# Unread identity products in the planned pauses of TensorE: a complex linear attention with a feed-forward behind it

## The chip, the cores and the metric

One core of one Trainium2 chip runs the whole program. The metric is the time of one execution in device microseconds (us). The kernel before took 697.37 us in the median of three runs (697.04 to 699.15). One more execution was profiled; every row of a trace below is from that one.

## The reference

For 4 batches and 8 heads, a state of 48x48 complex numbers runs over 768 time steps, and its output is the input of a two-layer feed-forward with GELU:

```python
mag = np.sqrt(a_re * a_re + a_im * a_im)
scale = np.minimum(mag, 0.999) / (mag + 1e-06)
a_re_n, a_im_n = (a_re * scale, a_im * scale)
for t in range(S):
    new_re = ar * S_re - ai * S_im
    new_im = ar * S_im + ai * S_re
    S_re, S_im = (new_re + kv, new_im)          # kv = k v^T of step t
    y[:, :, t] = np.einsum('bhd,bhde->bhe', q[:, :, t], S_re)
...
h = x @ w_in                                    # x: 3072 x 384, w_in: 384 x 2048
g = 0.5 * h * (1.0 + erf(h * inv_sqrt2))
return (g @ w_out).astype(np.float32)           # w_out: 2048 x 384
```

## The kernel before, in words

The recurrence is cut into chunks of time. The work has these parts, and the code names each of them:

- **lanes** (`tick`, `normalise`, `scan`, `squares_a`, `squares_b`, `logs`, `towards`, `against`): the factors `a` are normalised and multiplied up along time, slice by slice, in four groups of chunks. It is mostly work of VectorE (DVE) and ScalarE (ACT); its tiles are `a`, `tab`, `bt`, `tt` and `xt`. In the first group, `sum_of` lets TensorE (PE) add two squares: two products with the identity into a PSUM tile `att`, which ACT and DVE read. The results go to DRAM as `kq`.
- **weights** (`weights`): 32 pieces of the two weight matrices, 64-bit numbers that are split into a high part (`wi_hi`, `wo_hi`) and a low part (`wi_lo`, `wo_lo`). For each piece, PE subtracts in PSUM: identity times the rounded number, minus the high part, minus a correction. These three products in a row are called a triple here. Each triple goes into columns 0 to 383 of the same PSUM tile, `pos[BLK - 1]` (`po2`, one bank of 512 columns), and ACT or DVE copies the result out as `wi_lo` or `wo_lo`. So each triple must wait for the copy of the triple before it.
- **units** (`unit`): the attention of 128 time steps of one batch: loads of `kqn` and `vn`, transposes, scores, products with the state. The first two units come before the first block.
- **blocks** (`block`): the feed-forward, for two or three units at a time: `first` (`ph<-xT,wi_hi` and `wi_lo`), GELU on ACT, `second` (`po<-wo_hi,gh` and so on). Block `j0` is the first, `j1` the second. While a block is computed, the lanes, the weights and the units that later blocks need run beside it.

Nothing is issued as it is written: `Plan` records every operation as a step, and `Plan.order` puts the steps in order with a table of costs. Each step gets a planned engine, `s.start` and `s.cost`. `Plan.issue` (line 390) then issues them in that order, from one line, L399. So each engine has one fixed row of instructions, and each instruction waits in the row until what it needs is done. Waits between the engines are put in by the framework when an instruction is issued: it orders what touches the same tile where one of the two writes, and the rows in the section on the change show that it does so for `po2` as a whole, whatever columns of the bank are meant.

The planner doubles its cost of a PE step for some time after a pause, since PE runs at half of its clock then (`COLD`, `WARM` in `forward`). The planned times are used for nothing but the order.

The line of the code on which much of what follows rests, in `weights`, is:

```python
p = pos[BLK - 1][:, 0:DM]
```

Of the kernel before, what the change touches and what calls it, by code (L numbers as in the profile page):

```python
# [33 lines left out]
DM = H * D  # L34
# [4 lines left out]
BLK = max(BLOCKS)  # L39
# [45 lines left out]
TABLES = {AF.Ln: "natural_log_exp_and_others", AF.Exp: "natural_log_exp_and_others", AF.Gelu: "gelu"}  # L85
FIRST_TABLE = TABLES[AF.Ln]
NEAR = 0.076
LOCK = True
NGA, NGB = 4, 3
UPE = 6  # L90
# [18 lines left out]
class Plan:  # L109
# [78 lines left out]
    def ports(self, step, engine, calls):  # L188

        for call in calls:  # L190
            ins = [x for x in self.operands(call)[1] if x.tensor.space != PSUM and math.prod(c for _, c in x.ap[1:]) > 1]
            outs = self.operands(call)[0]
            if engine == "gpsimd" and ins or engine == "vector" and LOCK and (
                    len(ins) > 1 or ins and call[1] in ("tensor_scalar", "tensor_copy") and outs[0].tensor.space != PSUM):
# [79 lines left out]
    def forward(self, rank):  # L274
# [14 lines left out]
        while len(order) < len(steps):  # L289
            best = None  # L290
            for e, waiting in pool.items():
                if not waiting:
                    continue
                t = max(free[e], min(ready[i] for i in waiting)) + NEAR
                fits = [i for i in waiting if ready[i] <= t]
# [50 lines left out]
    def backward(self, end, taken, _):  # L346
# [8 lines left out]
        for _ in steps:  # L355
            best = None
            for e, waiting in pool.items():
                if not waiting:
                    continue
                t = min(free[e], max(ready[i] for i in waiting)) - NEAR  # L360
                i = last(i for i in waiting if ready[i] >= t)
# [25 lines left out]
            s.engine, s.start, s.cost, s.calls = e, start, cost, s.options[e][0]  # L387
        return [steps[i] for i in order]

    def issue(self):  # L390
        table = FIRST_TABLE
        self.nc.scalar.preload_act_table_set(table)
        for s in self.order():
            if s.table and s.table != table:
                table = s.table
                if table != "gelu":
                    self.nc.scalar.preload_act_table_set(table)  # L397
            for engine, name, args, kw in s.calls:
                getattr(getattr(self.nc, engine), name)(*args, **kw)  # L399

# [9 lines left out]
def lanes_and_chunks(ctx, tc, flags, a_lanes, x_lanes, v_units, w_in, w_out, out):  # L410
    nc = tc.nc
# [4 lines left out]
    P = Plan(nc, loose=[flags])  # L416
# [10 lines left out]
    ident = ident_r.bitcast(F32)  # L427
# [38 lines left out]
    pos = [ps.tile([128, 512], F32, name=f"po{i}", tag=f"po{i}")[:] for i in range(BLK)]  # L466
# [536 lines left out]
    for j, more in enumerate(BLOCKS[1:] + (0,)):  # L1003
# [6 lines left out]

        with P.work("blocks", f"j{j}"):
            block(j, between)
    P.issue()


def from_float64(nc, pool, src, out):
# [136 lines left out]
def tile_complex_linear_attention_moe(ctx, tc, q, k, v, a_re, a_im, w_in, w_out, a_lanes, x_lanes, v_units, w_pieces, out):  # L1153
# [9 lines left out]
    with ExitStack() as fast:  # L1163
        fast.enter_context(tc.manual_schedule())
        lanes_and_chunks(fast, tc, flags, a_lanes, x_lanes, v_units, w_pieces, w_out, out)
# [81 lines left out]
```

## Time and profile before

| | before |
|---|---|
| median of three runs | 697.37 us |
| profiled execution | 697.16 us |
| its span, from the first to the last instruction | 695.1 us |
| busy: PE, DVE, ACT | 638.8, 465.7, 459.3 us |
| mean granted clock of PE | 0.957 |

The 2.06 us between the span and the profiled execution's time are outside the program's instructions. PE is busy for 92% of the span, and the page's slices show where it isn't: in the first sixth. A row of a timeline gives the start, the time from the first to the last of a group, the engine, the line, the operation, what it writes and reads, its shapes, how many, and in brackets how long the engine sat idle before it and what it waited for. The products that take 32-bit numbers as they are (`po<-wh`, `att<-qT,kp`) leave two records each, the others one. Records of PE overlap, so the time of a piece of work is read from its start to the start of what follows at once.

### The profile page before, as it was taken

To read this page: it belongs to the slowest core of one execution; us is meant where nothing else is said; L and a number is where in the kernel's file an instruction comes from. 1 tells how busy PE (TensorE), PEld (TensorE's weight loads), DVE (VectorE), ACT (ScalarE), POOL (GpSimd) and SP (SyncE) were. 2 spreads that over 40 slices of the span, in tenths; PEclk is the share of its full clock that TensorE was granted. 3 is DMA by queue.
4 is the path that set the end of the run, shared out by engine and by line. 5 is a ranking of instruction groups with operands and counts; after the bars stand their busy time and mean duration, and the time that the engine had idled before them with its cause. 6 is when DMAs were issued, how large, how long until landed. Compare 5 with 4: busy or idle time off the path is not lost.

```text
span 695.1 us, 13858 instructions
## 1 busy us (share of the span) xinstructions
PE 638.8 (92%) x5138; PEld 588.3 (85%) x5138; DVE 465.7 (67%) x1154; ACT 459.3 (66%) x1118; POOL 31.9 (5%) x73
## 2 busy tenths in 40 slices
PE   3464799998999999999999999999999999999995
PEld 1232477996889999999889999999999999999995
DVE  5999988999999999999999973442332222131111
ACT  7777867999988788889899864454344333343332
POOL 1002110020000000300000000100000000000000
PEclk9865589999999999999999999999999999999998
DMA  8446936677455546637767555202322030010000
GB/s 303 138 136 176 301 110 165 203 199 234 134 150 148 148 119 183 180 95 217 206 198 212 118 133 149 83 20 72 113 76 61 5 103 1 1 44 4 24 1 26
DMA packets 112713, 86.68 MB, mean 125 GB/s; under 512 B 55680, under 2 KB 104960, under 8 KB 112640
## 3 DMA queue, kind: packets, MB, share of 16 engines
q1 hardware_dynamic: 112640, 85.75, 43.3%
q8 instruction: 41, 0.67, 0.4%
q14 instruction: 32, 0.26, 0.1%
HBM read 56.82 MB, written 23.59 MB: 116 GB/s over the span
## 4 chain that ended last, share of the span: by engine, by line
PE 75%; ACT 11%; DVE 10%; issue 2%; DMA 1%; SPq 0%; ACTq 0%; DVEq 0%
PE po L399 28%; PE ph L399 26%; PE att L399 20%; DVE a L399 2%; ACT tab L399 2%; DVE tt L399 1%; ACT wh L399 1%; ACT a L399 1%; DVE wh L399 1%; DVE xt L399 1%; ACT L399 1%; ACT L397 1%; DVE bt L399 1%; DVE tab L399 1%; ACT gh L399 1%
## 5 line engine op out<-in xcount | busy, mean ns | idle before, releaser
L399 PE MATMUL ph<-xT,wi_hi 128*128 128x384 f32 (+1 forms) x864 | 210.9, 326 | 0.3 <-ACT gf L399 0.3
L399 DVE TENSOR_TENSOR gl<-gf,gh 128x384 fp32r<-128x384 f32 (+1 forms) x143 | 72.9, 510 | 137.4 <-ACT gf L399 134.7
L399 PEld LDWEIGHTS ph<-xT,wi_hi 128*128 128x128 f32 x864 | 153.0, 188 | 3.1 <-ACT gf L399 0.6
L399 ACT ACTIVATE gh<-ph 128x384 fp32r<-128x384 f32 (+1 forms) x144 | 65.5, 455 | 134.3 <-PE ph L399 133.3
L399 PE MATMUL ph<-xT,wi_lo 128*128 128x384 f32 (+1 forms) x432 | 137.2, 318 | 1.8 <-ACT wi_lo L399 1.8
L399 PE MATMUL po<-wo_hi,gh 128*128 128x384 f32 x384 | 133.0, 346 | 1.1 <-ACT gh L399 0.9
L399 PE MATMUL po<-wo_lo,gh 128*128 128x384 f32 x384 | 129.6, 338 | 0.0
L399 PE MATMUL po<-wo_hi,gl 128*128 128x384 f32 x384 | 92.1, 341 | 0.3 <-DVE gl L399 0.3
L399 PEld LDWEIGHTS ph<-xT,wi_lo 128*128 128x128 f32 x432 | 81.2, 188 | 2.0 <-ACT wi_lo L399 2.0
L399 PEld LDWEIGHTS po<-wo_hi,gh 128*128 128x128 f32 x384 | 72.1, 188 | 3.4 <-ACT gh L399 2.5
L399 PEld LDWEIGHTS po<-wo_lo,gh 128*128 128x128 f32 x384 | 72.3, 188 | 0.1
L399 DVE TENSOR_TENSOR tt<-bt,a 128x192 f32<-128x192 f32 x192 | 69.0, 360 | 0.8
L399 PEld LDWEIGHTS po<-wo_hi,gl 128*128 128x128 f32 x384 | 65.9, 188 | 1.3 <-DVE gl L399 0.9
L399 ACT ACTIVATE gf<-ph 128x384 f32<-128x384 f32 (+1 forms) x144 | 65.0, 452 | 2.1 <-DVE gl L399 1.8
L399 PE MATMUL po<-wh,ident_r 128*128 128x384 f32 x64 | 35.4, 642 | 24.7 <-ACT wh L399 8.8
L399 PE MATMUL att<-qT,kp 96*128 96x128 f32 x384 | 53.4, 283 | 2.9 <-ACT kp L399 1.0
L399 DVE TENSOR_TENSOR kp<-att,causal 128x512 f32<-128x512 f32 x48 | 33.0, 687 | 30.8 <-PE att L399 30.0
L399 PEld LDWEIGHTS att<-qT,kp 96*128 96x128 f32 x384 | 48.8, 194 | 5.1 <-ACT qT L399 1.7
L399 DVE TENSOR_TENSOR bt<-tt 128x96 f32<-128x96 f32 x192 | 48.3, 251 | 0.9
L399 PEld LDWEIGHTS po<-wh,ident_r 128*128 128x128 f32 x64 | 12.6, 233 | 30.5 <-ACT wh L399 8.7
L399 PE MATMUL att<-ident_r,kqn 128*96 128x128 f32 x384 | 35.6, 237 | 0.3 <-DVE kp L399 0.2
L399 PEld LDWEIGHTS att<-ident_r,kqn 128*96 128x96 f32 x384 | 32.6, 127 | 3.1 <-DVE kp L399 0.5
(161 smaller groups left out, 1001.3 us busy)
## 6 DMA issues: line engine op xcount, KB each, us to landing
kqn<-kq SPq DMA_DIRECT2D x24, 768.0 KB, 5.1
xt<-in_x_lanes_dram SPq DMA_DIRECT2D x24, 384.0 KB, 3.7
kq<-xt SPq DMA_DIRECT2D x48, 192.0 KB, 3.8
kq<-xt SPq DMA_DIRECT2D x24, 384.0 KB, 4.1
a<-in_a_lanes_dram SPq DMA_DIRECT2D x20, 384.0 KB, 3.7
raw<-in_w_pieces_dram SPq DMA_DIRECT2D x16, 384.0 KB, 4.0
raw<-in_moe_w_out_dram SPq DMA_DIRECT2D x16, 384.0 KB, 3.9
vn<-in_v_units_dram SPq DMA_DIRECT2D x24, 256.0 KB, 5.4
```

Of the source, the lines that this page charges most:

```text
L397: self.nc.scalar.preload_act_table_set(table)
L399: getattr(getattr(self.nc, engine), name)(*args, **kw)
```

## The change

`issue` gets a function, `unread`, and calls it before a step of PE as often as the planned pause ahead of that step holds, less 0.1 us, at 0.23 us apiece. It stops at the first step of PE that belongs to block `j1`. The function issues one product, identity times identity, 128x128, in 32 bits, into columns 384 to 511 of the tile `po2`. These columns are set to zero once, by VectorE, and nobody reads them. The planner itself isn't touched: all steps keep their engines and their order.

```diff
+SPARE, UNREAD = 0.1, 0.23
...
-    def issue(self):
+    def issue(self, unread):
+
+        free, early = 0.0, True
...
+            if s.engine == "tensor":
+                early = early and s.part != "j1"
+                for _ in range(int((s.start - free - SPARE) / UNREAD) if early and free else 0):
+                    unread()
+                free = s.start + s.cost
             for engine, name, args, kw in s.calls:
...
-    P.issue()
+    unread = pos[BLK - 1][:, DM:512]
+    nc.vector.memset(unread, 0.0)
+    P.issue(lambda: nc.tensor.matmul(out=unread, lhsT=ident[:], rhs=ident[:], start=False, stop=False, skip_group_check=True))
```

164 such products are issued, in 20 groups of 4, 3, 12, 2, 19, 6, 22, 10, 19, 7, 19, 6, 8, 9, 3, 2, 3, 1, 6 and 3, in this order. In the rows below they are the lines with L1024; the other steps' line is L399 before and L407 after. The names: `po_115` is the tile `po2`, `wh` the rounded weight, `wi_hi`, `wi_lo`, `wo_hi`, `wo_lo` the parts of the split, `a_124` a slice of the lanes, `vw` the ends of a group of lanes. In brackets stands which engine's progress an instruction waits for.

The first place is PE's row at the last sum of squares of the first lanes (`att_110<-a_124`) and the triples around it. Before:

```order
29 L399 MATMUL po_115<-wh_120,ident_r 128x384 [waits DVE_49,Activation_49]
30 L399 MATMUL po_115<-wi_hi,minus 128x384
31 L399 MATMUL po_115<-wi_lo,minus 128x384 [waits DVE_49]
32 L399 MATMUL att_110<-a_124,ident_r 128x384 [waits Activation_49]
33 L399 MATMUL att_110<-a_124,ident_r 128x384 [waits DMAHW7_49]
34 L399 MATMUL po_115<-wh_121,ident_r 128x384 [waits DVE_49]
35 L399 MATMUL po_115<-wo_hi,minus 128x384 [waits Activation_49]
36 L399 MATMUL po_115<-wo_lo,minus 128x384 [waits DVE_49]
37 L399 MATMUL po_115<-wh_120,ident_r 128x384 [waits Activation_49]
```

and after the change, in the same place:

```order
41 L407 MATMUL po_115<-wh_120,ident_r 128x384 [waits DVE_49]
42 L407 MATMUL po_115<-wi_hi,minus 128x384
43 L407 MATMUL po_115<-wi_lo,minus 128x384 [waits DVE_49]
44 L1024 MATMUL po_115<-ident_r 128x128 [waits Activation_49]
45 L1024 MATMUL po_115<-ident_r 128x128 x21
46 L407 MATMUL att_110<-a_124,ident_r 128x384 [waits Activation_49]
47 L407 MATMUL att_110<-a_124,ident_r 128x384 [waits DMAHW7_49]
48 L1024 MATMUL po_115<-ident_r 128x128 x10
49 L407 MATMUL po_115<-wh_121,ident_r 128x384 [waits DVE_49]
50 L407 MATMUL po_115<-wo_hi,minus 128x384 [waits Activation_49]
51 L407 MATMUL po_115<-wo_lo,minus 128x384 [waits DVE_49]
52 L1024 MATMUL po_115<-ident_r 128x128 [waits Activation_49]
```

Twenty-two products came between a triple and the sum of squares, and ten between that and the next triple. The first product behind a triple (rows 44 and 52) waits for ACT's copy of that triple, as the next triple did before (row 37).

The second place is PE's row from the end of the first lanes to the first unit (`ph_111<-vn_141,kqn_139`). Before:

```order
43 L399 MATMUL att_108<-ident_r,vw_133 96x128 [waits Pool_49]
44 L399 MATMUL att_108<-ident_r,vw_133 96x128
45 L399 MATMUL po_115<-wh_120,ident_r 128x384 [waits DVE_49,Activation_49]
46 L399 MATMUL po_115<-wi_hi,minus 128x384 [waits Activation_49]
47 L399 MATMUL po_115<-wi_lo,minus 128x384 [waits DVE_49]
48 L399 MATMUL po_115<-wh_121,ident_r 128x384 [waits DVE_49,Activation_49]
```

and after the change:

```order
61 L407 MATMUL po_115<-wo_lo,minus 128x384 [waits DVE_49]
62 L1024 MATMUL po_115<-ident_r 128x128 [waits Activation_49]
63 L1024 MATMUL po_115<-ident_r 128x128 x18
64 L407 MATMUL att_108<-ident_r,vw_133 96x128 [waits Pool_49]
65 L407 MATMUL att_108<-ident_r,vw_133 96x128
66 L407 MATMUL po_115<-wh_120,ident_r 128x384 [waits DVE_49]
67 L407 MATMUL po_115<-wi_hi,minus 128x384 [waits Activation_49]
68 L407 MATMUL po_115<-wi_lo,minus 128x384 [waits DVE_49]
69 L1024 MATMUL po_115<-ident_r 128x128 [waits Activation_49]
70 L1024 MATMUL po_115<-ident_r 128x128 x5
71 L407 MATMUL po_115<-wh_121,ident_r 128x384 [waits DVE_49]
```

The transposes of `vw`, which waited for GpSimd alone, now stand behind nineteen products that wait for a copy on ACT; the wait for ACT has moved from each triple to the first product ahead of it. On ACT, GpSimd and the DMA queue the rows are the same as before; DVE has the one memset more.

## Prediction

> **What bounds the kernel now.** I read the page first, then stretches, then what PE waited for, then PE's, ACT's and DVE's timelines up to 170 us. The page's slices (40 of 17.4 us, busy share in tenths; PEclk is the granted clock of PE in tenths):
>
> ```profile
> span 695.1 us, 13858 instructions
> PE   3464799998999999999999999999999999999995
> DVE  5999988999999999999999973442332222131111
> PEclk9865589999999999999999999999999999999998
> ```
>
> Five stretches show the same in numbers (length, busy us of PE, PE's weight loads, DVE, ACT and GpSimd with counts, granted clock, DMA):
>
> ```profile
> 11.00:83.00 72.00, 38.66 (x79) 19.71 (x78) 70.60 (x196) 55.11 (x134) 6.48 (x11) 0.71 0.66 196
> 83.00:120.00 37.00, 35.63 (x375) 28.73 (x375) 32.91 (x77) 28.34 (x76) 3.31 (x2) 0.83 0.50 144
> 120.00:400.00 280.00, 274.52 (x2458) 256.51 (x2457) 272.30 (x699) 251.11 (x579) 14.83 (x30) 1.00 0.62 172
> ```
>
> From 11 to 83 us DVE works 70.6 of 72 us: the first lanes on DVE set the pace, and PE is only half busy, at a clock of 0.71. From 83 us PE is hardly ever idle: 1.4 us up to 120, 5.5 us up to 400. So PE sets the pace from the first unit on, and two things count: when PE starts on that unit, and how much it then loses to the clock. The clock loss is (1 - 0.83) x 37 = 6.3 us between 83 and 120 us, and nothing from there to 400. That is what there is to win; anything before 83 us that comes late on PE, ACT or DVE is lost.
>
> PE's own pauses in the early part:
>
> ```profile
> 49.86 2.93 PE L399 MATMUL att<-a,ident_r 128*128 128x384 f32 x4 [5.12 <-ACT a L399]
> 52.58 1.49 PE L399 MATMUL po<-wh,ident_r 128*128 128x384 f32 x2
> ...
> 58.71 1.65 PE L399 MATMUL po<-wh,ident_r 128*128 128x384 f32 x2 [3.22 <-ACT wo_lo L399]
> ...
> 64.11 1.65 PE L399 MATMUL po<-wh,ident_r 128*128 128x384 f32 x2 [2.88 <-ACT wi_lo L399]
> ...
> 66.20 0.63 PE L399 MATMUL att<-ident_r,vw 128*96 128x128 f32 x2
> ...
> 74.26 1.65 PE L399 MATMUL po<-wh,ident_r 128*128 128x384 f32 x2 [3.00 <-ACT wi_lo L399]
> ...
> 77.11 1.65 PE L399 MATMUL po<-wh,ident_r 128*128 128x384 f32 x2 [0.57 <-ACT wo_lo L399]
> ...
> 83.15 1.95 PE L399 MATMUL ph<-vn,kqn 64*64 64x48 f32 x32
> ```
>
> The pauses ahead of the triples end with ACT's copy of the triple before (`wi_lo`, `wo_lo`). The copies, and what else on ACT counts:
>
> ```profile
> 48.10 0.46 ACT L399 CAST wi_lo<-po 128x384 fp32r<-128x384 f32 x1
> ...
> 52.89 0.58 ACT L399 ACTIVATE a<-att,by_partition 128x384 f32<-128x384 f32 x1 [1.93 <-PE att L399]
> ...
> 53.93 0.83 ACT L399 ACTIVATE tab<-a 128x768 f32<-128x768 f32 x1
> ...
> 58.20 0.46 ACT L399 CAST wo_lo<-po 128x384 fp32r<-128x384 f32 x1
> ...
> 69.44 0.36 ACT L399 COPY vwT<-att 96x256 f32<-96x256 f32 x1
> ```
>
> The copy that ends at 58.66 releases the triple at 58.71: the pause is the wait for the copy, to its end.
>
> **The change part by part.** The memset of the spare columns lies ahead of the first lanes on DVE, which has nothing to do then; I cost it at nothing. What is left is 164 products and their waits.
>
> A product's price comes from four products of 32-bit numbers of the same output size, at half and at full clock:
>
> ```profile
> 87.92 2.07 PE L399 MATMUL att<-qT,kp 96*128 96x128 f32 x8
> 89.65 1.20 PE L399 MATMUL att<-ident_r,kqn 128*96 128x128 f32 x8
> ...
> 128.59 1.12 PE L399 MATMUL att<-qT,kp 96*128 96x128 f32 x8
> 129.47 0.48 PE L399 MATMUL ph<-xT,wi_hi 128*128 128x256 f32 x2
> ...
> 135.40 0.81 PE L399 MATMUL po<-wh,ident_r 128*128 128x384 f32 x2
> ...
> 136.40 0.40 PE L399 MATMUL ph<-xT,wi_hi 128*128 128x256 f32 x2
> ```
>
> (89.65 - 87.92) / 4 = 0.43 us, and (129.47 - 128.59) / 4 = 0.22 us. A triple takes 136.40 - 135.40 = 1.00 us at full clock, and 77.11 - 0.57 - 74.26 = 2.28 us at half. I take the full clock for the products: with them PE works most of the time.
>
> The order in the section on the change decides the rest. The first product behind a triple waits for that triple's copy. So the products don't run in the pause, which is the wait for the same copy; they run behind it, and what stands behind them on PE comes later by all of them.
>
> *Up to 49 us* (groups 1 to 6, 46 products, 10.1 us). Here the pauses are partly waits for lanes, which give cover:
>
> ```profile
> PE att L399 <- ACT tab L399: 8.8, 3, 5.7
> ...
> PE att L399 <- ACT a L399: 7.9, 2, 5.1
> ```
>
> Without the 5.12 us at 49.86 these are 11.6 us, more than the products, but the groups start only after a copy. The lateness is between nothing and 4 us (four cold products at the start, 1.7 us, and a few more in the group of 19); I take 2.1 us on ACT and DVE.
>
> *The group of 22 and the 10 behind it.* The copy ends at 48.56, with the 2.1 us at 50.7. Then come 22 x 0.22 = 4.8 us, and the sum of squares, 2.72 us (52.58 - 49.86) at half clock and 1.4 at full: it ends at 56.9. ACT wanted it at 52.89, so ACT is 4.1 us late, and DVE, which needs ACT's `tab<-a` of 53.93, as well. The ten products (2.2) and a triple (1.0) end at 60.1, before ACT gets to its copy: 58.66 + 4.2 = 62.9.
>
> *From that copy to the first unit* it took 83.15 - 58.66 = 24.5 us. Now it holds 19 + 7 + 19 + 6 + 8 + 9 + 3 = 71 products, 15.6 us; six triples, 6.0; the transposes of `vw`, 0.4; and five copies, at least 0.55 each from a triple's end, 2.75. That is 24.75 us: all that the full clock saves on six triples is used up. So the unit starts 4.2 + 0.25 = 4.5 us late at the least. But ACT's row has `vwT` (69.44, with 4.3 us of lateness 73.7) ahead of the next copies, and `vw` now comes behind 19 products, at 76.0; ACT then stands for 2.5 us, and DVE for some time after it. Walking on row by row I get 91.2 for the unit, **+8.0 us**, and take that (bounds 4.5, and 11.5 with two restarts from half clock, below).
>
> *The first unit, 83.15 to 92.68* (9.53 us, the next rows): at full clock by the ratio 0.88 / 1.73 this is 4.9 us; 5 products add 1.1, and ACT's copies of the transposes, which were hidden behind a slow PE, about 1.0. Together 7.0: **-2.5 us** (bounds -3.6 and -1.5).
>
> ```profile
> 92.68 0.66 PE L399 MATMUL po<-kp,vn 128*64 128x128 f32 x8
> ...
> 111.82 1.13 PE L399 MATMUL att<-qT,kp 96*128 96x128 f32 x8 [0.97 <-ACT wh L399]
> ...
> 159.03 0.39 PE L399 MATMUL ph<-xT,wi_lo 128*128 128x256 f32 x1 [1.76 <-ACT wi_lo L399]
> ```
>
> *The second dip* of the clock, behind the pause at 111.82, costs 6.3 - (9.53 - 4.9) = 1.7 us. One product stands there; I take **-1.0** (0 to -1.7).
>
> *The last ten products* (1, 6 and 3): the six wait for the copy that ends the pause at 159.03, so they and the two products behind them come after it. 10 x 0.22 + 0.35: **+2.5** (1.0 to 3.0).
>
> *Given back later*: PE's 5.5 us of waits between 120 and 400 shrink only as far as ACT and DVE are less late than PE. They are about as late: **-1.5** (0 to -5.5).
>
> Sum: 8.0 - 2.5 - 1.0 + 2.5 - 1.5 = +5.5 us on the profiled execution's 697.16 (span 695.1 and 2.06 outside it), 0.21 us under the median of the runs shown. Forecast **702.7 us**.
>
> A rule of the Trainium skill (TensorE: Matmul & The Clock Gate, Part 1) speaks for this change: PE's clock falls to half after an idle window of about 3.4 us and comes back after a busy one. The rows agree that there are two speeds; but the triples after pauses of 2.88 and 0.57 us ran at half too, so short pauses alone don't keep the clock. By the rule alone (clock kept, products free) the sum would be that of the first rival.
> The same skill's PSUM — Partial Sum Buffer (Terms) calls it an error when PE writes a bank that ACT reads at that moment; no run here shows it, but it says why other columns of one bank don't free the products from the copy.
>
> **The rivals.**
> *The pauses hold the products, and the clock pays* (faster). If lateness before the first unit is nothing, the triples at full clock bring the unit forward by some 2 us; the unit gains 4.6 less 1.1 for its products, the dip 1.7: -7.2 us. DVE, 272.3 of 280 us busy later, can't follow all of it; with 4 us given back, 694. For it: the clock of 0.5 in the slices. Against it: row 44 of the order. It decides at the first unit: if PE starts there less than 2.5 us late, the sum is below zero. 0.17.
> *PE falls to half clock between the groups* (slower still). Behind the triples before the groups of 19 and 22 PE still waits for a copy, 3 to 4 us. It then starts cold: between 49.86 and 55 it ran slow for about 4 us, 9 products at 0.43 instead of 0.22, 1.9 us each time. Three times: 702.7 + 5.6 = 708.3. 0.15.
> *It evens out* (no change): the unit 4.5 us late, -3.6, -1.7, +1.0: 697.4. 0.12.
> That the products are not issued is excluded by the order.
>
> **How the numbers follow.** My forecast has 0.56. The forecast and the colder rival make slower, 0.71; the range goes from 696.5 (in it what evens out, without the faster rival) to 709.5 (above the colder one). 0.3%, about 2.1 us, is what a measurement of this kernel can tell from no change. Faster 0.17, same 0.12, slower 0.71.
>
> **What would show it.** In the changed kernel's timeline of PE: the first product of a group starts when ACT's copy ends; `att<-a` at 49.86 starts after 55; the first unit (`ph<-vn,kqn`) starts near 91; PE's clock from there on is 1.00. ACT's idle time before `a<-att` (1.93) grows to about 4, and it waits for `vw`. I am wrong if the unit starts before 85.6, or if DVE is not late there.

## The result, and the profile after

The changed kernel took 717.53 us in the median of four runs (714.8 to 721.51), the kernel before 697.67 us beside it. The ratio is 1.029 (95% interval 1.023 to 1.034): slower, and by 20 us instead of the forecast 5.5. The profiled execution took 717.2 us, 20.0 more than that of before, and the spans (715.1 and 695.1 us) differ by the same 20.0.

The page of the changed kernel, same slices:

```profile
span 715.1 us, 14505 instructions
...
PE   3768789998999999999989999999999999999995
...
DVE  5887869899999999999989994333332222131211
...
PEclk9998999999999999999999999999999999999998
```

The three stretches (length, busy us of PE, weight loads, DVE, ACT, GpSimd with counts, granted clock, DMA):

```profile
11.00:83.00 72.00, 54.26 (x307) 44.53 (x307) 60.39 (x165) 44.63 (x107) 3.94 (x6) 0.93 0.53 153
83.00:120.00 37.00, 31.05 (x299) 24.92 (x297) 29.98 (x76) 25.96 (x67) 4.34 (x6) 0.95 0.57 172
120.00:400.00 280.00, 272.28 (x2511) 252.17 (x2510) 266.41 (x680) 247.18 (x581) 15.93 (x31) 0.99 0.62 171
```

From 11 to 83 us PE is busier (54.3 us instead of 38.7) and its granted clock is 0.93 instead of 0.71. But DVE, which set the pace there, works 60.4 us instead of 70.6: it has become the one that waits. Read by the clock alone, this page looks like a success.

PE's timeline shows what the clock hides. A product leaves two records, so "x44" is the group of 22 and "x38" one of 19:

```profile
53.86 6.67 PE L1024 MATMUL po<-ident_r 128*128 128x128 f32 x44 [3.60 <-ACT wi_lo L407]
60.36 1.46 PE L407 MATMUL att<-a,ident_r 128*128 128x384 f32 x4
...
67.72 5.89 PE L1024 MATMUL po<-ident_r 128*128 128x128 f32 x38 [2.67 <-ACT wo_lo L407]
73.46 0.81 PE L407 MATMUL po<-wh,ident_r 128*128 128x384 f32 x2
...
86.97 2.26 PE L1024 MATMUL po<-ident_r 128*128 128x128 f32 x12 [2.48 <-ACT wi_lo L407]
89.02 1.49 PE L407 MATMUL po<-wh,ident_r 128*128 128x384 f32 x2
...
100.43 1.14 PE L407 MATMUL ph<-vn,kqn 64*64 64x48 f32 x32
...
107.88 0.66 PE L407 MATMUL po<-kp,vn 128*64 128x128 f32 x8
```

PE still waits 2.5 to 3.6 us ahead of these groups, for ACT's copy, and only then issues the products. And the products behind such a wait are dear: the group of 22 takes 60.36 - 53.86 = 6.50 us, 0.295 each, the group of 19 takes 73.46 - 67.72 = 5.74, 0.302 each. The forecast had 0.22. The first unit starts at 100.43, which is 17.3 us late and not 8.0.

ACT's timeline has the two waits that the prediction named:

```profile
53.34 0.46 ACT L407 CAST wi_lo<-po 128x384 fp32r<-128x384 f32 x1
61.91 0.58 ACT L407 ACTIVATE a<-att,by_partition 128x384 f32<-128x384 f32 x1 [5.71 <-PE att L407]
...
83.52 0.37 ACT L407 COPY vwT<-att 96x256 f32<-96x256 f32 x1 [2.65 <-PE att L407]
```

The copy ends at 53.80 and the first product starts at 53.86. `a<-att` waits 5.71 us for PE instead of 1.93, and `vwT` 2.65.

### The profile page after: what moved, and what is told of

It reads as the page before. It is cut to its first block, busy times and chain, and to the rows that moved or that the text cites. A ratio compares the mean times of both kernels' runs of the same rounds, so it can differ in the third digit from the quotient of the medians.

```text
span 715.1 us, 14505 instructions
## 1 busy us (share of the span) xinstructions
PE 667.2 (93%) x5466; PEld 624.5 (87%) x5466; DVE 466.4 (65%) x1155; ACT 459.3 (64%) x1118; POOL 31.5 (4%) x73
## 4 chain that ended last, share of the span: by engine, by line
PE 77%; ACT 12%; DVE 7%; issue 2%; DMA 1%; ACTq 0%; DVEq 0%; SPq 0%
PE po L407 28%; PE ph L407 26%; PE att L407 19%; PE po L1024 5%; ACT tab L407 2%; ACT wh L407 2%; DVE a L407 2%; ACT a L407 1%; DVE tt L407 1%; ACT L400 1%; ACT L407 1%; DMA m<-st 1%; DVE wh L407 1%; ACT gh L407 1%; DVE xt L407 1%
## 5 line engine op out<-in xcount | busy, mean ns | idle before, releaser
L407 PE MATMUL ph<-xT,wi_hi 128*128 128x384 f32 (+1 forms) x864 | 211.7, 327 | 0.3 <-ACT gf L407 0.3
L407 DVE TENSOR_TENSOR gl<-gf,gh 128x384 fp32r<-128x384 f32 (+1 forms) x143 | 73.0, 510 | 137.0 <-ACT gf L407 134.3
L407 PEld LDWEIGHTS ph<-xT,wi_hi 128*128 128x128 f32 x864 | 153.6, 189 | 3.1 <-ACT gf L407 0.6
L407 ACT ACTIVATE gh<-ph 128x384 fp32r<-128x384 f32 (+1 forms) x144 | 65.6, 456 | 134.8 <-PE ph L407 133.7
L407 PE MATMUL ph<-xT,wi_lo 128*128 128x384 f32 (+1 forms) x432 | 137.4, 318 | 0.0
L407 PE MATMUL po<-wo_hi,gh 128*128 128x384 f32 x384 | 132.9, 346 | 0.7 <-ACT gh L407 0.5
L407 PE MATMUL po<-wo_lo,gh 128*128 128x384 f32 x384 | 129.6, 338 | 0.0
L407 PE MATMUL po<-wo_hi,gl 128*128 128x384 f32 x384 | 92.1, 341 | 0.8 <-DVE gl L407 0.8
L407 PEld LDWEIGHTS ph<-xT,wi_lo 128*128 128x128 f32 x432 | 81.5, 189 | 0.0
L407 PEld LDWEIGHTS po<-wo_hi,gh 128*128 128x128 f32 x384 | 72.1, 188 | 2.5 <-ACT gh L407 1.7
L1024 PE MATMUL po<-ident_r 128*128 128x128 f32 x328 | 47.6, 306 | 26.6 <-ACT wi_lo L407 15.5
L407 PEld LDWEIGHTS po<-wo_lo,gh 128*128 128x128 f32 x384 | 72.3, 188 | 0.1
L1024 PEld LDWEIGHTS po<-ident_r 128*128 128x128 f32 x328 | 44.2, 216 | 32.0 <-ACT wi_lo L407 17.9
L407 DVE TENSOR_TENSOR tt<-bt,a 128x192 f32<-128x192 f32 x192 | 69.2, 360 | 0.8
L407 PEld LDWEIGHTS po<-wo_hi,gl 128*128 128x128 f32 x384 | 65.9, 188 | 1.8 <-DVE gl L407 1.4
L407 ACT ACTIVATE gf<-ph 128x384 f32<-128x384 f32 (+1 forms) x144 | 65.2, 453 | 2.8 <-DVE gl L407 2.8
L407 PE MATMUL att<-qT,kp 96*128 96x128 f32 x384 | 53.1, 282 | 1.2 <-ACT kp L407 1.0
L407 DVE TENSOR_TENSOR kp<-att,causal 128x512 f32<-128x512 f32 x48 | 33.0, 688 | 31.6 <-PE att L407 30.5
L407 PEld LDWEIGHTS att<-qT,kp 96*128 96x128 f32 x384 | 48.6, 193 | 3.1 <-ACT kp L407 1.2
L407 DVE TENSOR_TENSOR bt<-tt 128x96 f32<-128x96 f32 x192 | 48.5, 253 | 0.9
L407 PE MATMUL po<-wh,ident_r 128*128 128x384 f32 x64 | 29.2, 541 | 8.8 <-ACT wh L407 8.8
L407 PE MATMUL att<-ident_r,kqn 128*96 128x128 f32 x384 | 35.0, 234 | 1.8 <-DVE x L407 1.4
```

Of the source, the lines that this page charges most:

```text
L1024: P.issue(lambda: nc.tensor.matmul(out=unread, lhsT=ident[:], rhs=ident[:], start=False, stop=False, skip_group_check=True))
```

## The experiments

Ten more runs were made, one of them of the changed kernel once more. The line of the products is L1024, L1026, L1027 or L1029 in them, that of the other steps L407, L409, L410 or L411. Where a text counts lateness, it is the start of the same instruction on PE minus its start in the trace of before. This table, worked out so from PE's timelines, serves for all of them; its columns are named by when the instruction started before (the first unit; the unit's `po<-kp,vn`; then four products of the feed-forward) and the last is the difference of the spans:

| kernel | 83.15 | 92.68 | 129.90 | 177.41 | 335.91 | 378.87 | span |
|---|---|---|---|---|---|---|---|
| changed | +17.3 | +15.2 | +15.8 | +16.4 | +16.5 | +19.7 | +20.0 |
| changed, second trace | +18.7 | +16.6 | +17.2 | +19.5 | +19.5 | +22.2 | +22.1 |
| without the five in the unit | +16.5 | +15.5 | +15.3 | +17.6 | +17.6 | +18.5 | +18.2 |
| without the last ten | +19.3 | +17.3 | +17.3 | +17.3 | +17.3 | +17.2 | +17.2 |
| first 149 only | +19.3 | +18.3 | +18.1 | +18.1 | +18.2 | +17.9 | +17.5 |
| first 149, PE kept busy ahead | +9.5 | +7.9 | +7.9 | +7.9 | +8.2 | +7.9 | +7.8 |
| all 164, PE kept busy ahead | +9.2 | +7.1 | +7.7 | +10.1 | +10.3 | +12.4 | +12.4 |
| one product in each group | +1.7 | +0.7 | -0.2 | -0.2 | -0.1 | -0.4 | -0.6 |
| last 15 only | +1.3 | +2.9 | +3.5 | +5.8 | +5.8 | +5.5 | +5.3 |
| 149 in a free bank | -1.6 | -2.1 | -2.3 | -2.3 | -2.3 | -2.6 | -2.2 |
| trimmed, free bank | -2.6 | -2.0 | -3.5 | -3.4 | -3.4 | -2.4 | -2.5 |

Each row is one execution, and one execution differs from another by itself: with the last 15 only, nothing ahead of 83.15 is changed but the memset at the start, and its row has +1.3 there. So a difference of a microsecond between two rows says little alone.

My theory after the result: the products stand behind the copy, as predicted, and cost number times price; but where PE has waited more than some 2 us for the copy they mostly start at half clock, so the price was set too low. Rivals: the loss sits in the late products; a product simply costs more in this place; the wait itself is the cost; the load on PE is, wherever the products write.

### The first 149 products only

```diff
-                for _ in range(int((s.start - free - SPARE) / UNREAD) if early and free else 0):
+                n = int((s.start - free - SPARE) / UNREAD) if early and free else 0
+                group += n > 0
+                for _ in range(n if group <= 15 else 0):
                     unread()
```

> Only the first 149 products are issued, those up to the first unit; the last 15 are left out. Theory (the products stand behind the copy of the triple, and where PE has waited for that copy for more than about 2 us they also start at half clock): the loss is all made before the first unit, so that unit again starts 16 to 18 us late and the time is 714 to 717. Rival (the loss beyond the forecast of 702.7 comes from the late products, in the units and after them): the unit starts about as late, but the time falls to 709 or less.

Measured: 713.32 us, ratio 1.019 (1.014 to 1.024). The unit starts as late as expected or later (102.40, +19.3), so most of the loss is made before it. The time lies between the two bounds: by the ratios (1.019 against 1.029 for the whole change) the last 15 products are worth some 6.6 us, and neither theory had that. PE's timeline of this kernel:

```profile
68.10 6.14 PE L1026 MATMUL po<-ident_r 128*128 128x128 f32 x38 [2.67 <-ACT wo_lo L409]
74.07 0.81 PE L409 MATMUL po<-wh,ident_r 128*128 128x384 f32 x2
...
102.40 1.14 PE L409 MATMUL ph<-vn,kqn 64*64 64x48 f32 x32
```

### The same 149, with PE kept busy ahead of the groups

The numbers in `AHEAD` are products into the free tile `po0`, which don't wait for the copy; the group itself stays in `po2`.

```diff
+AHEAD = {1: 8, 5: 12, 6: 11, 7: 14, 9: 11, 12: 9, 14: 6}
...
+                ahead = AHEAD.get(group, 0)
+                for i in range(n + ahead if n > 0 and group <= 15 else 0):
+                    unread(i < ahead)
```

> The 149 products of the run that stops at the first unit, into the same bank as before, and 71 more ahead of seven of the groups, into another tile that nothing uses then, as many as fit at 0.22 into the wait that was seen there (12 into 3.0 us, 11 into 2.7, 14 into 3.6). Theory of the cold start: the groups behind now start at full clock, a group of 19 takes 4.2 us instead of 5.9, and with 71 products more the first unit starts 4 to 8 us earlier than without them, at +9 to +13; time 707 to 712. Rival (a product in this place simply costs 0.27 to 0.31, whatever the clock): the unit starts as late as without them or later, time 715 or more.

Measured: 704.95 us, ratio 1.008 (1.006 to 1.011), below the 707 expected at the least; the unit is 9.5 us late, inside the +9 to +13. With 71 products more the kernel is 8.4 us faster than without them. The same groups in its timeline of PE:

```profile
50.30 5.18 PE L1029 MATMUL po<-ident_r 128*128 128x128 f32 x44 [0.49 <-ACT wi_lo L411]
55.32 1.46 PE L411 MATMUL att<-a,ident_r 128*128 128x384 f32 x4
...
62.69 4.51 PE L1029 MATMUL po<-ident_r 128*128 128x128 f32 x38 [0.24 <-ACT wo_lo L411]
67.04 0.81 PE L411 MATMUL po<-wh,ident_r 128*128 128x384 f32 x2
...
92.66 1.14 PE L411 MATMUL ph<-vn,kqn 64*64 64x48 f32 x32
```

The group of 19 takes 4.35 us instead of 5.97, 0.229 each, because PE was idle for only 0.24 us ahead of it. The unit starts at 92.66 instead of 102.40. So half clock behind the waits is shown to cost 9.7 us at the unit and 8.4 us of the time. That a product simply costs 0.3 in this place is out.

### The same 149 in a free bank

```diff
-    unread = pos[BLK - 1][:, DM:512]
+    unread = pos[0][:, DM:512]
```

(and the cut at 149 as above)

> The same 149 products go into columns 384 to 511 of another PSUM tile, po0, which nothing uses before the first unit; so none of them waits for a copy. Theory: with the wait gone they run in the pauses (the group of 19 is 4.2 us at 0.22, in waits of 3 to 5 us), the first unit starts -1 to +3 us against before instead of +17, at full clock, and the time is 691 to 697. Rival (the price is the load of 149 products on PE, wherever they write): the unit still starts 8 us late or more and the time is above 703.

Measured: 695.15 us, ratio 0.9945 (0.992 to 0.997): faster than before. Its stretch from 11 us on, and PE's timeline:

```profile
11.00:83.00 72.00, 61.10 (x415) 51.13 (x414) 71.47 (x198) 56.00 (x137) 6.06 (x11) 0.98 0.69 202
```

```profile
44.43 5.96 PE L1026 MATMUL po<-ident_r 128*128 128x128 f32 x44
50.24 1.46 PE L409 MATMUL att<-a,ident_r 128*128 128x384 f32 x4
...
64.60 4.40 PE L1026 MATMUL po<-ident_r 128*128 128x128 f32 x38
68.84 0.38 PE L409 MATMUL att<-ident_r,vw 128*96 128x128 f32 x2
...
81.51 1.14 PE L409 MATMUL ph<-vn,kqn 64*64 64x48 f32 x32
...
86.44 1.36 PE L409 MATMUL att<-qT,kp 96*128 96x128 f32 x8 [2.05 <-ACT qT L409]
```

No group of products has a wait in brackets: they follow at once on the work ahead and lie in the pause. DVE is as busy as before (71.5 us), and the unit starts 1.6 us early instead of 17 to 19 late. The number of products is the same as in the first experiment; only the bank differs. So the wait for the copy, with the work behind it, is what makes the change slow; the load on PE is not. Tile and bank are the same thing here, and the wait is one that the framework puts in for the tile (row 44 of the order); what the bank alone would do without that wait, no run shows. A row that still shows harm is `vw` at 68.84 (66.20 before), behind 19 products.

### One product in each group

```diff
-                for _ in range(n if group <= 15 else 0):
+                for _ in range(min(n, 1) if group <= 15 else 0):
```

> One product in each of the 15 groups up to the first unit, into the same bank: all the waits of the change, with a tenth of its products. Theory (the cost is number times price, the wait itself costs little since the triple behind it waits for the same copy anyway): the first unit starts 0 to 2 us late, time 697 to 699.5. Rival (the wait itself holds up the sums of squares and the transposes behind it): 4 us late or more, time above 701.

Measured: 696.91 us, ratio 0.998 (0.996 to 1.001): no change that can be told. Its timeline of PE:

```profile
58.52 0.80 PE L1026 MATMUL po<-ident_r 128*128 128x128 f32 x2 [3.22 <-ACT wo_lo L409]
...
84.80 1.15 PE L409 MATMUL ph<-vn,kqn 64*64 64x48 f32 x32
```

All the waits are there (3.22 us ahead of one product), and the unit is 1.7 us late. The wait costs next to nothing by itself; the products behind it do.

### The changed kernel once more, and the last 15 alone

The first is the changed kernel without any edit. The second has `group > 15` in place of `group <= 15`.

> The changed kernel itself once more, unaltered, for a second trace of it. In its first trace 3.2 us were lost between 330 and 372 us, behind a load of the state that took 4.9 us, and the kernel without the last 15 products lost nothing there. Theory (that loss is an accident of one execution): PE's lateness is the same at the first unit and at the end, within 1 us, and the time is 713 to 718. Rival (the loss there belongs to the change): the end is 3 us later than the first unit again, and the time is 717 or more.

> Only the last 15 products, those in the first units and behind them, where PE is hardly ever idle; the 149 ahead of them are left out. The forecast had 1.1 us for the five in the unit and 2.5 us for the ten behind it. Theory: they cost at most their time at full clock, 1 to 3 us, time 698 to 701. Rival (PE's waits in that place hide them, and the start of the first unit alone decides): within 1 us of before.

Measured: 718.44 us (ratio 1.030, 1.027 to 1.033) and 702.36 us (ratio 1.007, 1.004 to 1.010). The last 15 alone cost 5.5 us by the medians (702.36 - 696.82), above both bounds; with the 14.8 of the first 149 by theirs (713.32 - 698.55) that is 20.3, about the whole of the loss. (In the table 1.3 of their 5.3 us are there before the first of them is issued.) The loss behind 330 us that I took for an accident came again in the second trace, 2.7 us instead of 3.2, in other instructions.

Where the 15 cost: in the table, 1.5 us in the unit and 2.3 us between 129.90 and 177.41. There stand the six products behind the wait for a copy. The same group of six in the changed kernel, in its second trace, and in the kernel with the last 15 alone:

```profile
174.80 1.60 PE L1024 MATMUL po<-ident_r 128*128 128x128 f32 x12 [2.01 <-ACT wi_lo L407]
```

```profile
176.16 2.16 PE L1024 MATMUL po<-ident_r 128*128 128x128 f32 x12 [2.00 <-ACT wi_lo L407]
```

```profile
162.52 2.67 PE L1026 MATMUL po<-ident_r 128*128 128x128 f32 x12 [2.01 <-ACT wi_lo L409]
```

The same instructions behind the same wait of 2.0 us take 1.60, 2.16 and 2.67 us. At this length of wait it differs from one execution to the next how much of the group runs at half clock.

### The premise made true, and the last 15 in two parts

The first kernel has the products ahead of the groups (`AHEAD`) and all 164 products. The second stops at `group <= 17`, so the ten behind the unit are left out; the third has `group not in (16, 17)`, so the five in the unit are.

> All 164 products of the change in their places and their bank, and the 71 in a free tile ahead of seven groups that kept PE warm in the earlier run: the premise of the forecast, products at full clock, made true. Theory (the forecast of 702.7 failed by this premise, and by some 3 us more in the last 15 products and behind them): the first unit starts 9 to 10 us late, the time is 706 to 710. Rival (with the clock kept the steps of the forecast hold as they are): 704.5 or less.

> The change without its last ten products (groups of 1, 6 and 3 behind the first unit). Theory (they stand behind waits and cost 0.6 to 2.3 us in the traces; the rest of the 5 us that the last 15 cost comes from the five in the unit): 715 to 717, and the loss between 330 and 372 us is gone, as it is with all 15 left out. Rival (the loss there comes with the lateness of PE before the unit, and the ten have nothing to do with it): 717 or more, with 2 us or more lost there.

> The change without the five products inside the first unit. In the changed kernel the unit took 7.45 us with them and without any of the last 15 about 9 us, at half clock; so the five may keep the clock as well as cost their time. Theory (they pay for themselves): 717 to 719, the unit from its start to its first products with the state over 8.5 us. Rival (they cost their time, 1 to 2 us): 715 to 716.5, the unit no longer than 7.5 us.

Measured: 708.94 us (ratio 1.017, 1.012 to 1.022), 712.82 (1.021, 1.020 to 1.023) and 717.43 (1.030, 1.027 to 1.033).

With the clock kept up to the unit, the change costs 1.7% instead of 2.9 to 3.0%: some 8 to 9 us of the loss are the clock ahead of the unit, and the 11 to 12 us that remain are still twice the forecast.

Without the ten, 5 to 6 us are gone by the ratios (1.021 against 1.029 and 1.030); the theory gave them 1 to 3 and is too low, while its other half came true: nothing is lost behind 330 us. In the table their kernel is flat from 129.90 to the end. Each of the five traces with the ten is later at 177.41 than at 129.90 (by 0.6 to 2.4), and four of them lose 0.9 to 3.2 us more between 335.91 and 378.87. Without the ten five of six lose nothing there (the trimmed kernel lost 1.0).

Without the five nothing is gained (ratio 1.030, as with them). Here is why, from its timeline of PE:

```profile
103.34 2.08 PE L409 MATMUL att<-qT,kp 96*128 96x128 f32 x8 [0.85 <-ACT qT L409]
```

The scores of the unit run at half clock again, in 2.08 us; with the five they took 1.06. The stretch from the unit's start to `po<-kp,vn` is 8.6 us without the five and 7.45 with them. They pay for themselves.

### A version that beats both

All products into the free tile, the groups cut or lengthened to what was left of the waits, 154 in all (the numbers in `FIT`; the 145 of the expectation are those without the nine in the unit):

```diff
+FIT = {1: 8, 2: 3, 3: 12, 4: 2, 5: 14, 6: 16, 7: 20, 8: 8, 9: 14, 10: 12, 11: 9, 12: 12, 13: 6, 14: 9, 17: 9}
...
+                for _ in range(FIT.get(group, 0) if n > 0 else 0):
+                    unread()
...
-    unread = pos[BLK - 1][:, DM:512]
+    unread = pos[0][:, DM:512]
```

> A version that is meant to beat both: 145 products, all into the free tile po0, none behind a wait for a copy; the groups are cut or lengthened to what fits at 0.22 into the wait that was left in the run with the other bank, the one right before the first unit and the one inside it are dropped, and nine stand ahead of the first scores of the unit, where PE sat idle for 2.05 us and came back at half clock. Theory: the first unit starts 2 to 4 us before its old time, its first scores run at full clock, time 690 to 694. Rival (DVE, 71.5 of 72 us busy, sets the start of the unit, and no filling of PE's pauses brings it forward any more): the unit starts where it did in the other run, at about -1.6, and the time is 694 to 696.

Measured: 694.13 us, ratio 0.9956 (0.994 to 0.998). It beats the kernel before, and the simple version with the free bank (0.9945) just as much; the fitting was worth nothing that can be measured. PE's timeline in its first unit:

```profile
80.58 1.14 PE L410 MATMUL ph<-vn,kqn 64*64 64x48 f32 x32
...
83.27 1.14 PE L410 MATMUL po<-vn,kqn 64*64 64x48 f32 x32 [0.86 <-DMA kqn<-kq]
84.33 3.90 PE L1027 MATMUL po<-ident_r 128*128 128x128 f32 x18
88.07 1.06 PE L410 MATMUL att<-qT,kp 96*128 96x128 f32 x8
```

The unit starts 2.6 us early, but then waits 0.86 us for a load, and my nine products ran at half clock, 3.74 us instead of 2.0. The scores behind them, at full clock (1.06), start at 88.07, later than in the free-bank kernel, where they started at 86.44. So both halves of the expectation came: an earlier unit, and no gain. What bounds the start of the unit then was not tried further.

## Why the prediction was wrong

*The order, and what waits behind it: right.* The first product starts 0.06 us after the copy ends; `att<-a` starts at 60.36 (after 55, as announced); ACT waits 5.71 and 2.65 us for it and for `vw`. That the wait alone costs next to nothing was shown by the kernel with one product each, and that without the wait the same products cost nothing by the one with the free bank.

*"I take the full clock for the products: with them PE works most of the time." This is the step that failed.* The products could not fill the waits that I had just shown to lie ahead of them, so PE was idle for 2.3 to 3.6 us, six times before the unit. I used a mean over the stretch where each group's own history counts. In the changed kernel the groups at 13.29, 35.09, 53.86 and 67.72 and the six with their triple at 86.97 (five of the six places; behind the 2.70 us at 47.66 the six ran at full clock) took 0.9, 1.6, 1.5, 1.4 and 1.4 us more than the same work in the kernel where PE was kept busy ahead. Already the copy that I had put at 50.7 ended at 53.80; with PE kept busy ahead the first product behind it started at 50.30. At the unit that made +17.3 (and +18.7) of the predicted +8.0; with the clock kept it was +9.2 and +9.5, inside my bounds of 4.5 to 11.5. My bounds took only two restarts in.

*The rival "PE falls to half clock between the groups" had the mechanism, with too few restarts*: three at 1.9 us, 5.6 us. Measured were five at 0.9 to 1.6 us in one trace, and in time 8.4 us for the first 149 and 8 to 9 for all.

*The first unit, -2.5 (-3.6 to -1.5): right*, -2.1 in both traces of the changed kernel.

*The second dip of the clock, -1.0 (0 to -1.7): wrong in sign*, +0.6 in both traces from 92.68 to 129.90. One product stands behind a wait of 1.3 us there and doesn't fill it.

*The last ten, +2.5 (1.0 to 3.0)*: at their own place +0.7 in the first trace and +2.3 in the four others that have them. But leaving them out is worth 5 to 6 us of the time, with what goes with them behind 335.91 (below).

*Given back later, -1.5 (0 to -5.5): failed.* Nothing came back up to 335.91, since DVE and ACT were as late as PE, and 3.2 and 2.7 us were lost behind it. What PE waits for there, in the first trace:

```profile
355.85 0.47 PE L407 MATMUL att<-ident_r,kqn 128*96 128x128 f32 x4 [1.36 <-DVE x L407]
...
360.59 1.91 PE L407 MATMUL att<-qT,kp 96*128 96x128 f32 x8 [1.01 <-ACT kp L407]
```

and in the second:

```profile
358.47 0.47 PE L407 MATMUL att<-ident_r,kqn 128*96 128x128 f32 x4 [0.95 <-DVE x L407]
...
363.21 1.16 PE L407 MATMUL att<-qT,kp 96*128 96x128 f32 x8 [1.02 <-ACT kp L407]
```

In the first the scores ran at half clock as well (1.91 against 1.16). It goes with the last ten products, in four of the five traces that have them, but how products at 127 to 180 us make a wait at 355 longer is not settled.

With the clock kept up to the unit, all 164 products lost on the profiled execution 9.2 - 2.1 + 0.6 + 2.4 + 0.2 + 2.1 = 12.4 us by the columns of the table, against the forecast +5.5: of the 6.9 between them 3.8 stand in "given back later" (+2.3 for -1.5), 1.6 in the dip, 1.2 in the start of the unit, 0.4 in the unit, and -0.1 in the ten.

## What to carry to other kernels

Filler work keeps an engine's clock only if it can run in the pause: see what its first instruction waits for, and if that is what the pause itself waits for, the filler stands behind the pause and is paid in full, and in part at half clock. Write fillers to memory that no other engine reads or writes in that time; the same 149 products cost 2% in the shared bank and gained half a per cent in a free one. And price work by the idle time in the microseconds ahead of it, not by the mean clock of the stretch, and as a range: the slow part of it moves from one execution to the next.

## What was unexpected of the hardware

Neither how long a wait costs PE its clock nor when is a fixed number here. Behind 2.67 and 3.60 us a product of the groups of 19 and 22 took 0.302 and 0.295 us on average, against 0.229 and 0.228 behind 0.24 and 0.49 us. But such a group need not start slow. The changed kernel's group of 19 behind 3.00 us, cut in three stretches (the third number from the end of a row is the granted clock):

```profile
35.09:36.55 1.46, 1.46 (x13) 1.46 (x14) 1.46 (x5) 0.50 (x1) 0.00 (x0) 0.99 0.96 274
36.55:39.95 3.40, 3.40 (x18) 3.40 (x17) 3.40 (x11) 2.08 (x5) 0.00 (x0) 0.50 0.32 87
39.95:41.07 1.12, 1.12 (x12) 1.12 (x11) 1.12 (x5) 0.42 (x1) 0.00 (x0) 1.00 1.08 339
```

PE is busy throughout, runs at full clock for 1.5 us, then at half for 3.4, then at full again. And the group of eight behind only 0.57 us, 4 to 5 us after a wait of 2.5 us had ended, in the first and the second trace of the changed kernel:

```profile
91.72 2.05 PE L1024 MATMUL po<-ident_r 128*128 128x128 f32 x16 [0.57 <-ACT wo_lo L407]
```

```profile
91.24 3.78 PE L1024 MATMUL po<-ident_r 128*128 128x128 f32 x16 [0.57 <-ACT wo_lo L407]
```

In the second it ran at half clock from end to end, which goes into that trace's +18.7. Behind 2.0 us it is mixed too: the same group of six took 1.60 to 2.67 us in the five traces that have it. So the slow part can come behind the wait, in the middle of busy work, or only behind the next short wait. The Trainium skill (TensorE: Matmul & The Clock Gate, Part 1) calls the window by which the clock is decided free-running, so that the count of slow products varies from run to run; the spread of the group of six agrees. It puts that window at about 3.4 us; here a wait of 2.67 us was enough for a group that ran in part at half clock, and the measurement decides.
